# A mixed product scheme for the branch products of a Mamba-2 / merge kernel: three token blocks of 512 and two of 768, weight sums added up by DMAs, order by a list scheduler

## The chip, the cores and the metric

The kernel runs on one core of a Trainium2 chip. The metric is the device time of one execution in microseconds (us). Engines: PE (matmuls; PEld is its weight load), DVE (VectorE), ACT (ScalarE), POOL (GpSimd), SP (SyncE, which here only issues DMAs). Everything is float32.

## The reference, cut to what matters

First a state-space attention: 4 sequences of 768 tokens, 8 heads of 32 columns, state size 16. Its output becomes x, 3072 tokens by 256 columns. Then four branches are merged:

```
p = domain_probs / (domain_probs.sum(-1, keepdims=True) + 1e-09)
for e in range(4):
    h = np.maximum(x @ w1[e], 0.0)           # 256 -> 1024
    out += p[:, e:e + 1] * (h @ w2[e])       # 1024 -> 256
```

## The kernel before

The tokens are 24 chunks of 128, taken in turn from the four sequences. A block is 4 chunks (512 tokens), and there are 6 blocks. The FFN of a block runs over 8 steps (4 branches by 2); a step takes 512 of a branch's 1024 hidden columns. "First" products multiply by w1, "second" products by w2. In pieces of 256 hidden columns, 256 tokens and 128 model columns a step is a 2x2 times 2x2 block matrix product, twice. Instead of 8 block products it makes 7, by Strassen's method in Winograd's form (`fmul`, `smul`). One block product is two matmul instructions of 128x128 by 256 columns, and each float32 matmul leaves two records in the trace.

The price of the saved products is sums on other engines:
- of tokens, four of 128x256 per block on DVE (`sums`, L501 to L504);
- of weights, on POOL in block 0 (`sums_of`, L189 to L193); they are stored in DRAM by DMAs from POOL (L201, L207) and loaded from there by SP in later blocks (L166 and L177 are the loads' lines in `load_w1` and `load_w2`, beside those of the plain weights, L161 and L173);
- of first products: partial results are copied out of a bank by ACT (`snap`, L530), added to another bank by DVE (`total`, L535), then made non-negative and multiplied by the gate p (`gated`, L545);
- of gated results, four differences per step on DVE (`diff`, L552);
- of second products, once per block (`combine`). They stay in four PSUM banks (`acc`) for a whole block.

The first two steps of block 0 (`PLAIN = 2`) use 8 plain products, in `plain_first` (L572) and `plain_second` (L589).

The attention of the next block is woven in. Per chunk: two scans on DVE (`decay_part`, L364), scores on PE (L393), a product with the decays on DVE (`masked`, L405), a small product on POOL that fades the state (L369), for later chunks another on POOL (`cts`, L350), outputs on PE (L450, L462), and copies on ACT.

The order of all of this is written by hand: a loop over n = 2 ... 47 issues one step's first products between the second products of the step before (`fmul`, `smul`). Each engine takes its instructions in that order. SP issues nearly all loads two steps ahead. `finish` writes the end: the last second products in an order of their own, with each result added straight out of its bank, turned by PE and sent.

Of the kernel before, what the change touches and what calls it, by code (L numbers as in the profile page):

```python
# [12 lines left out]
P = 128  # L13
NQ, NT = 4, 2


@with_exitstack
def kernel(
# [10 lines left out]

# [3 lines left out]
    E, DM, F = w1.shape  # L60
    NH = NQ * NT
    HN = P
    BLK = 512
    HB = BLK // 2
    CPB = BLK // P
    NBLK = NCH // CPB
# [4 lines left out]
    FH = F // 2  # L71
    JJ = FH // HB
    SPB = E * JJ
    NS = NBLK * SPB
    assert NBLK == chunks_per_seq

    def real(c):

        return c % CPB * NBLK + c // CPB

    PLAIN = 2
    A12, A22, A11, S3, S1, S2, S4 = range(7)

    const = ctx.enter_context(tc.tile_pool(name="const", bufs=1))
    load = ctx.enter_context(tc.tile_pool(name="load", bufs=3))
    wts = ctx.enter_context(tc.tile_pool(name="wts", bufs=3))
    att = ctx.enter_context(tc.tile_pool(name="att", bufs=2))
    ffn = ctx.enter_context(tc.tile_pool(name="ffn", bufs=2))
    ps_att = ctx.enter_context(tc.tile_pool(name="ps_att", bufs=2, space=bass.MemoryType.PSUM))
    ps_f = ctx.enter_context(tc.tile_pool(name="ps_f", bufs=1, space=bass.MemoryType.PSUM))  # L90
    ps_s = ctx.enter_context(tc.tile_pool(name="ps_s", bufs=1, space=bass.MemoryType.PSUM))
    ctx.enter_context(tc.manual_schedule())


    ac_d = tc.dram_tile([NCH, NH, P], FP32, name="ac_d")
    acut_d = tc.dram_tile([NCH, NH, P], FP32, name="acut_d")
    p_d = tc.dram_tile([T // P, E, P], FP32, name="p_d")
    w1_d = [tc.dram_tile([P, 4, HB], FP32, name=f"w1_d{i}") for i in range(SPB)]
    w2_d = [tc.dram_tile([P, 5 * HB], FP32, name=f"w2_d{i}") for i in range(SPB)]


    st = {}
    SPREAD = 3

    HALF = P // 2

    def turned_round(c):


        return c >= CPB and c % 2 == 1  # L110

    def load_tokens(c):
        xb = load.tile([P, W], FP32, tag="xb", name="xb", bufs=4)
        src = xbc[real(c)]
        if turned_round(c):
            nc.sync.dma_start(out=xb[:, :OBT], in_=src[:, :OBT])
            nc.sync.dma_start(out=xb[:HALF, OBT:], in_=src[HALF:, OBT:])
            nc.sync.dma_start(out=xb[HALF:, OBT:], in_=src[:HALF, OBT:])
        else:
            nc.sync.dma_start(out=xb, in_=src)  # L120
        st.setdefault(c, {})["xb"] = xb

    def load_rows(c):

        xb = load.tile([P, W], FP32, tag="xb", name="xb", bufs=4)
        nc.sync.dma_start(out=xb[:, OBT:], in_=xbc[real(c)][:, OBT:])
        st.setdefault(c, {})["xb"] = xb

    def load_rest(c):
        nc.sync.dma_start(out=st[c]["xb"][:, :OBT], in_=xbc[real(c)][:, :OBT])  # L130

    def load_decays(c):
        ab = load.tile([P, NH * P], FP32, tag="ab", name="ab")
        nc.sync.dma_start(
            out=ab, in_=acut_d[real(c)].rearrange("h s -> (h s)").partition_broadcast(P))
        st.setdefault(c, {})["ab"] = ab

    def load_heads(c):

        ah = st[c]["ah"] = load.tile([HN, P], FP32, tag="ah", name="ah", bufs=4)  # L140
        src = ac_d[real(c)].unsqueeze(1).to_broadcast([NH, N, P])
        if turned_round(c):
            nc.sync.dma_start(out=ah[:HALF], in_=src[NH // 2:])
            nc.sync.dma_start(out=ah[HALF:], in_=src[:NH // 2])
        else:
            nc.sync.dma_start(out=ah, in_=src)

    def load_chunk(c):
        load_tokens(c)
        load_decays(c)  # L150
        load_heads(c)

    wt1, wt2 = {}, {}

    def load_w1(n):
        e, jj = divmod(n % SPB, JJ)
        t1 = wt1[n] = wts.tile([P, 7, HB], FP32, tag="wt1", name="wt1", bufs=5)
        for k in range(2):
            w = 2 - 2 * k
            a_ = 2 if n < SPB or k else 1  # L160
            nc.sync.dma_start(  # L161
                out=t1[:, w:w + a_],
                in_=w1[e, k * P:k * P + P].rearrange("p (a f) -> p a f", a=2)[
                    :, 0:a_, jj * HB:jj * HB + HB])
        if n >= SPB:
            nc.sync.dma_start(out=t1[:, S3:], in_=w1_d[n % SPB])  # L166

    def load_w2(n):
        e, jj = divmod(n % SPB, JJ)
        t2 = wt2[n] = wts.tile([P, 7 * HB], FP32, tag="wt2", name="wt2", bufs=5)  # L170
        for i in range(2) if n < SPB else (1,):
            f = i * FH + jj * HB
            nc.sync.dma_start(  # L173
                out=t2[:, (1 - i) * 2 * HB:(2 - i) * 2 * HB].rearrange("p (j m) -> p j m", j=JJ),
                in_=w2[e, f:f + HB].rearrange("(j p) m -> p j m", p=P))
        if n >= SPB:
            nc.sync.dma_start(out=t2[:, 2 * HB:], in_=w2_d[n % SPB])  # L177

    def w2_op(n, w):

        if w < 4:
            a_, d = divmod(w, 2)
            return wt2[n][:, :4 * HB].rearrange(
                "p (a j d m) -> p a j d m", a=2, j=JJ, d=2)[:, a_, :, d]
        return wt2[n][:, w * HB:w * HB + HB].rearrange("p (j m) -> p j m", j=JJ)

    def sums_of(op, part):
        if part != 1:
            nc.gpsimd.tensor_add(op(S1), op(S3), op(A22))  # L189
            nc.gpsimd.tensor_sub(op(S2), op(S1), op(A11))  # L190
            nc.gpsimd.tensor_sub(op(S4), op(A12), op(S2))
        if part != 0:
            nc.gpsimd.tensor_sub(op(S3), op(A11), op(S3))  # L193

    def sum_w1(n, part=None):


        if n < SPB:
            sums_of(lambda w: wt1[n][:, w].rearrange("p (j m) -> p j m", j=JJ), part)
            if part != 0:  # L200
                nc.gpsimd.dma_start(out=w1_d[n], in_=wt1[n][:, S3:])  # L201

    def sum_w2(n, part=None):
        if n < SPB:
            sums_of(lambda w: w2_op(n, w), part)
            if part != 0:
                nc.gpsimd.dma_start(out=w2_d[n], in_=wt2[n][:, 2 * HB:])  # L207

    pr = const.tile([P, T // P, E], FP32, name="pr")
    a_sb = const.tile([NCH * NH // 2, 2, P], FP32, name="a_sb")  # L210

    a_q = ffn.tile([P, SPREAD, NT, P], FP32, tag="o", name="a_q", bufs=1)
    nc.gpsimd.memset(a_q[:, 0], 0.0)
    one = nc.const_aps.tensor(1.0, [P, 1])
    nc.vector.memset(a_q[:, 1:], 0.0)
    nc.scalar.dma_start(out=pr, in_=probs)
    for queue, c in ((nc.sync, slice(0, 1)), (nc.scalar, slice(1, SPREAD))):
        queue.dma_start(
            out=a_q.rearrange("(q r) c t s -> q r c (t s)", q=NQ)[:, 0, c],
            in_=a.rearrange("(i k) (q t) s -> k q i (t s)", k=NBLK, t=NT)[0][:, c])  # L220
    warm = const.tile([P, 1], FP32, name="warm")
    nc.scalar.mul(warm, one, one)
    load_rows(0)
    nc.sync.dma_start(
        out=a_sb, in_=a.rearrange("c h s -> (c h) s").rearrange("(p r) s -> p r s", r=2))
    load_rows(1)
    load_rest(0)
    load_rest(1)
    load_w1(0)
    load_tokens(2)  # L230


    ident = const.tile([P, NQ, P], FP32, name="ident")
# [4 lines left out]
    tmask = const.tile([P, NT], FP32, name="tmask")  # L238
# [5 lines left out]
    zeros = const.tile([P, P], FP32, name="zeros")  # L244
    nc.vector.memset(zeros, 0.0)

    qmask = const.tile([P, NQ, D], FP32, name="qmask")
# [3 lines left out]

    own = const.tile([P, 1], FP32, name="own")
# [6 lines left out]


    def clip_first(engine, c):
        clip(engine, a_q[:, c].rearrange("p c t s -> p (c t s)"), own)
        engine.memset(a_q[:, c, :, 0:1], 0.0)

    clip_first(nc.vector, slice(0, 1))


    pairs = const.tile([P, T // P, 2], FP32, name="pairs")
# [4 lines left out]

    nc.vector.reciprocal(total_p, total_p)
    nc.gpsimd.tensor_mul(pr, pr, total_p.to_broadcast([P, T // P, E]))
    clip_first(nc.vector, slice(1, SPREAD))

    clip(nc.gpsimd, a_sb)

# [9 lines left out]
    gate = {}  # L289

    def turn_gates(pool, tag):

        rows = T // P * E
        pp = pool.tile([rows, P], FP32, tag=tag, name="pp")
        nc.tensor.transpose(pp, pr.rearrange("p i e -> p (i e)"), ident[:, 0])
        p_sb = const.tile([rows, P], FP32, name="p_sb")
        gate["rows"] = p_sb
        nc.scalar.copy(out=p_sb, in_=pp)  # L298

    def store_gates():  # L300
        nc.sync.dma_start(out=p_d.rearrange("i e s -> (i e) s"), in_=gate["rows"])

    def spread_gate(pool, tag):

        p_sb = gate["rows"]
        g = pool.tile([P, CPB, P], FP32, tag=tag, name="gp")
        for i in range(CPB):
            r = real(i) * E
            nc.tensor.matmul(  # L309
# [663 lines left out]
```

## Time and profile before

| | |
|---|---|
| three timed runs | 637.74, 638.09, 638.25 us |
| median | 638.09 us |
| span of the profiled execution, first to last instruction | 636.4 us |
| ACT busy in the span | 119.7 us |
| POOL busy in the span | 112.9 us |
| moved by DMA | 121.61 MB, mean 191 GB/s |
| granted TensorE clock | 1.000 |

The span is that of one execution under the profiler, and its own time outside the span is not listed, so 638.09 - 636.4 = 1.7 us is taken for what lies around it. A group line names the line of the code, the engine, the operation, output <- inputs, the shape and a count; then busy us, mean ns of one, and the idle time of the engine just before, with what ended it. Durations of matmuls overlap, because they are pipelined: the distance between starts is their price.

### The profile page before, as it was taken

What the parts mean: (1) busy time and instruction counts of PE and PEld (TensorE: products, weight loads), DVE (VectorE), ACT (ScalarE), POOL (GpSimd) and SP (SyncE); (2) the same over time, 40 slices, a digit from 0 to 9 for tenths busy, and PEclk for the clock granted to TensorE, in tenths of its full rate; (3) what the DMA queues carried; (4) which work ended last, traced back from release to release, by engine and by line L of the source; (5) the groups of instructions that cost most, each with busy time, mean ns of one, the idle gap of its engine ahead of it and who ended that gap; (6) DMA issues with size and microseconds to landing.
All of it is one profiled execution on the core that took longest, in us unless ns stands there. A gap on an engine that the chain in (4) does not pass through costs nothing.

```text
span 636.4 us, 9259 instructions
## 1 busy us (share of the span) xinstructions
PE 631.9 (99%) x3405; PEld 538.2 (85%) x3405; DVE 483.4 (76%) x810; ACT 119.7 (19%) x264; POOL 112.9 (18%) x164
## 2 busy tenths in 40 slices
PE   9999999999999999999999999999999999999997
PEld 5888888888888888888888888888888888888886
DVE  7868999887787788678687778778867677756555
ACT  4011221212111221122211221122111211111110
POOL 6788557020000002000002000000100000100001
PEclk9999999999999999999999999999999999999999
DMA  6998894745666392757284566639365644167001
GB/s 188 302 357 295 282 346 156 279 169 166 191 200 238 90 366 81 228 175 248 99 287 149 168 199 196 231 102 358 89 220 162 242 160 133 61 152 241 2 1 33
DMA packets 98513, 121.61 MB, mean 191 GB/s; under 512 B 29529, under 2 KB 81957, under 8 KB 98469
## 3 DMA queue, kind: packets, MB, share of 16 engines
q1 hardware_dynamic: 95512, 111.20, 53.7%
q0 software_dynamic: 2432, 9.50, 3.8%
q8 instruction: 27, 0.44, 0.3%
q10 hardware_dynamic: 524, 0.32, 0.2%
q14 instruction: 18, 0.14, 0.1%
HBM read 108.16 MB, written 12.83 MB: 190 GB/s over the span
## 4 chain that ended last, share of the span: by engine, by line
PE 99%; ACT 0%; DVE 0%; issue 0%
PE acc L608 44%; PE X L523 25%; PE Y L523 19%; PE acc L589 2%; PE g L393 2%; PE y L462 2%; PE X L572 1%; PE Y L572 1%; PE y L450 1%; PE t L729 1%; PE a L331 0%; PE y L428 0%; PE gp L309 0%; PE turned L655 0%; DVE o L686 0%; ACT p_sb L298 0%
## 5 line engine op out<-in xcount | busy, mean ns | idle before, releaser
L535 DVE TENSOR_TENSOR z<-Y,snap 128x512 f32<-128x512 f32 x138 | 94.6, 686 | 117.6 <-ACT snap L530 66.7
L608 PE MATMUL acc<-hT,wt 128*128 128x256 f32 x736 | 181.1, 379 | 0.0
L530 ACT COPY snap<-X 128x512 f32<-128x512 f32 x138 | 80.8, 586 | 464.2 <-PE X L523 403.5
L608 PEld LDWEIGHTS acc<-hT,wt 128*128 128x128 f32 x736 | 140.1, 190 | 18.7
L608 PE MATMUL acc<-h,wt 128*128 128x256 f32 x552 | 142.6, 381 | 0.0
L523 PE MATMUL X<-yS,wt 128*128 128x256 f32 x552 | 141.8, 380 | 0.0
L608 PEld LDWEIGHTS acc<-h,wt 128*128 128x128 f32 x552 | 104.2, 190 | 16.8 <-issue 2.3
L523 PEld LDWEIGHTS X<-yS,wt 128*128 128x128 f32 x552 | 105.0, 190 | 14.3 <-issue 0.3
L545 DVE SCALAR_TENSOR_TENSOR h<-z,gate 128x512 f32<-128x512 f32 x138 | 99.9, 724 | 3.5 <-PE acc L589 0.4
L523 PE MATMUL Y<-yT,wt 128*128 128x256 f32 x368 | 94.5, 379 | 0.0
L523 PEld LDWEIGHTS Y<-yT,wt 128*128 128x128 f32 x368 | 68.9, 190 | 10.5
L552 DVE TENSOR_TENSOR hT<-h,hT 128x512 f32<-128x512 f32 x92 | 65.2, 709 | 1.8
L552 DVE TENSOR_TENSOR hT<-h,h 128x512 f32<-128x512 f32 x92 | 65.1, 748 | 1.4
L364 DVE TENSOR_TENSOR_SCAN LT<-ab,ident 128x512 f32<-128x512 f32 x42 | 52.1, 1242 | 0.0
L523 PE MATMUL Y<-yS,wt 128*128 128x256 f32 x184 | 48.3, 385 | 0.0
L523 PE MATMUL X<-yT,wt 128*128 128x256 f32 x184 | 47.3, 379 | 0.0
L369 POOL TENSOR_TENSOR MT<-xb,LT 128x128 f32<-128x128 f32 x20 | 8.6, 428 | 205.4 <-PE Y L523 68.8
L405 DVE TENSOR_TENSOR MT<-g,LT 128x256 f32<-128x256 f32 x93 | 32.0, 415 | 11.5 <-PE g L393 11.4
L523 PEld LDWEIGHTS Y<-yS,wt 128*128 128x128 f32 x184 | 34.2, 190 | 6.4 <-issue 2.2
L523 PEld LDWEIGHTS X<-yT,wt 128*128 128x128 f32 x184 | 35.0, 190 | 4.7
L545 DVE SCALAR_TENSOR_TENSOR h<-X,gate 128x512 f32<-128x512 f32 x50 | 34.2, 684 | 5.0 <-PE X L523 3.4
L350 POOL TENSOR_TENSOR cts<-ctm,dec 128x256 f32<-128x256 f32 x20 | 14.1, 726 | 128.3 <-DVE dec L347 128.3
(103 smaller groups left out, 325.2 us busy)
## 6 DMA issues: line engine op xcount, KB each, us to landing
wt<-in_w_dram SPq DMA_DIRECT2D x112, 256.0 KB
wt<-w_d SPq DMA_DIRECT2D x40, 640.0 KB
wt<-w_d SPq DMA_DIRECT2D x40, 512.0 KB
ab<-acut_d SPq DMA_DIRECT2D x21, 512.0 KB
gate<-p_d SPq DMA_DIRECT2D x23, 256.0 KB
w_d<-wt POOLq DMA_DIRECT2D x8, 640.0 KB, 3.7
wt<-in_w_dram SPq DMA_DIRECT2D x40, 128.0 KB
w_d<-wt POOLq DMA_DIRECT2D x8, 512.0 KB, 7.7
```

Of the source, the lines that this page charges most:

```text
L350: nc.gpsimd.tensor_mul(cts, s["ctm"], dec.unsqueeze(1).to_broadcast([HN, NT, P]))
L364: nc.vector.tensor_tensor_scan(out=LT[:, i * w:i * w + w], data0=s["a"][i], data1=ident.rearrange("p h s -> p (h s)")[:, :w], initial=0.0, ...
L393: nc.tensor.matmul(out=g.rearrange("p t s -> p (t s)"), lhsT=s["xb"][k, OBT:OBT + P], rhs=s["ctm"][k].rearrange("p t s -> p (t s)"), start ...
L405: nc.vector.tensor_mul(s["MT"][:, h, 0:P], s["g"][q], s["LT"][:, h])
L462: nc.tensor.matmul(out=y[32 * q:32 * q + 32, t, 0:w], lhsT=s["xb"][:, h * D:h * D + D], rhs=s["MT"][:, NT * q + t, 0:w], start=(k == 0 and ...
L523: nc.tensor.matmul(out=f[bank][:, j], lhsT=wt1[n][:, w, j * P:j * P + P], rhs=rhs, start=(i in (1, 2, 5) and j == 0), stop=(j == JJ - 1), ...
L530: nc.scalar.copy(out=s, in_=first[n]["X"])
L535: nc.vector.tensor_add(z, first[n]["Y"], first[n][i])
L545: nc.vector.scalar_tensor_tensor(out=h, in0=first[n][src], scalar=0.0, in1=g.unsqueeze(1).to_broadcast([P, JJ, HB]), op0=ALU.max, op1=ALU. ...
L552: nc.vector.tensor_sub(h[o], h[x], h[y])
L572: nc.tensor.matmul(out=f[bank][:, j], lhsT=wt1[n][:, w, j * P:j * P + P], rhs=yT[k][:, i, cols], start=(i == 0 and j == 0), stop=(i == 1), ...
L608: nc.tensor.matmul(out=acc[k, u][:, half], lhsT=w2_op(n, w)[:, j], rhs=rhs[:, j], start=(begins and j == 0), stop=(n % SPB == SPB - 1 and ...
```

## The change

Lines with L from here on are those of the changed kernel.

- **Blocks.** 24 chunks become three blocks of 4 chunks (scheme `B`, 2x2x2 in 7 products for 8) and two of 6 chunks (scheme `H`). `H` takes 768 hidden columns and 768 tokens at a time, 3x2 pieces of weights times 2x3 of tokens and back, in 15 products for 18, with 10 sums of weights, 12 of tokens, and in each group 7 sums with a bank and 16 of SBUF tiles. A branch pair's 1024 x 4 columns are 16 pieces of 256: five groups of three, and piece 0 plainly. Block 0 has 4 pieces (one branch) plainly.
- **Banks.** All 8 banks are one pool. A running sum is continued in a bank that ACT fills first (`seed`, L837), and saved by ACT (`snap`, L832; `visit`, L1096 and L1099). Second products no longer keep four banks for a block: `visit` takes one bank for a "house" of two results, seeds it, adds the products of that group, and copies it back to SBUF.
- **Weight sums.** Those of `B` are made on DVE or POOL (L930) and stored by SP (L935). Those of `H` are made in DRAM: a DMA of SP copies one summand (L893), then a DMA of POOL adds the other (L896, L901; a sum of sums waits for the one before). Ten chains (5 groups by 2 weights) of ten sums go one by one with the 11 units of the first three blocks. A unit is two groups of `B` or one of `H`.
- **Order.** Each operation is entered in a `Plan` with its engine (some with DVE or POOL), an expected duration, what it reads and writes. PE's order is given: first products of a unit interleaved with second products of the unit before (`put`), scores after the unit's first product (SC = 1) and outputs after the 14th (OUT = 14). `Plan.run` fills the other engines by due time, gives out the buffers and the banks, and decides DVE or POOL. The instructions are issued in the order of planned starts.
- **End.** The last group's second products run alone, by house (`LATE`); each house is copied to SBUF and the results are added there, turned by PE and sent (`leave_last`).
- The products' line is L823, the gates' L858, other sums of large tiles L850, L976, L1001 and L1146, the fading product L454, `cts` L731, scores L436, outputs L461 and L767, weight loads L411, L417 and L927.

```diff
-    ORDER = (1, 3, 7, 5, 6, 2, 4)
...
-    for n in range(PLAIN, NS):
...
-        opened(n)
-        total(n, 1, "11")
-        gated(n, "11", "z11")
...
+ORDER = B, B, B, H, H
...
+    def add(self, on, fn, reads=(), writes=(), part=(), lag=0.0, due=None, reuse=None, two=False,
+            port=True, after=None):
...
+            e = min(t, key=lambda e: t[e])
+            now = t[e]
...
+                if len(w.on) > 1 and e == "POOL":
+                    if max(ready, now) + w.on[e] > w.latest + late + SLACK or self.backlog(
+                            waiting["DVE"], now, t["DVE"], w) < BACK:
+                        continue
+                rank = w.latest
...
+    homes = {
+        "V": some(NV, [P, 2, FB], "v"),
+        "W": some(NW, [P, 2 * FB], "w"),
+        "bank": some(8, [P, 512], "bank", psum),
...
+    def product(bank, half, w, x, start):
+
+        for j in range(JJ):
+            o = bank.rearrange("p (a m) -> p a m", a=2)[:, j if half is None else half]
+            nc.tensor.matmul(
+                out=o, lhsT=w[:, j], rhs=x if half is None else x[:, j],
+                start=(start and j == 0), stop=(j == 1), skip_group_check=True)
...
+    def sums_by_dma(scheme, fbs, l, after, due):
...
+            dma(lambda e, r=r, f=f, i=i: nc.sync.dma_start(
+                out=split(slot[r]), in_=source(fbs[f], l, i)), 1, 300, writes=[v], due=due, after=after)
+            if y in sums:
+                plan.add({"POOL": 1.0}, lambda e, r=r, y=y: nc.gpsimd.dma_start(
+                    out=slot[r], in_=slot[y], accum_op=ALU.add), port=False, lag=ACC,
+                    reads=[sums[y]], part=[v], due=due, after=after)
+            else:
+                g, h = scheme.blocks[l][y]
+                plan.add({"POOL": 1.0}, lambda e, r=r, g=g, h=h: nc.gpsimd.dma_start(
+                    out=split(slot[r]), in_=source(fbs[g], l, h), accum_op=ALU.add), port=False,
+                    lag=ACC, part=[v], due=due, after=after, reads=[v])
...
+    def threes_first(k, fbs):
...
+        b7 = mul(7)
+        s7 = snap(b7)
+        s12 = snap(mul(12))
+        mul(11, b7)
+        a12 = combine(b7, s12, -1)
+        gate(2, 0, mul(0, seed(s7)))
+        b6 = mul(6)
+        t67 = combine(snap(b6), s7, -1)
+        b3 = mul(3)
+        s3 = snap(b3)
+        b5 = mul(5, seed(a12))
+        gate(2, 2, b5)
+        mul(2, b7)
+        gate(1, 2, combine(b7, s12, -1))
+        mul(10, b3)
+        v = combine(b3, s12, -1)
...
+    def visit(k, house, terms, last=False):
...
+        bank = seed(held, size) if held is not None else value("bank", fills=both)
...
+        v = kept[k, house] = value("V")
+        v.both = both
+        if both:
+            act(.6, lambda e: nc.scalar.copy(out=flat(v), in_=bank.t), reads=[bank], writes=[v])
...
+    def leave_last(k, O, order):
...
+            tails.append(plan.add({"PE": .35}, turn, reads=[o], writes=[t]))
+            act(.4, lambda e, t=t, r=r: nc.scalar.copy(out=r.t[:, 0], in_=t.t[:, :2 * P]),
+                reads=[t], writes=[r])
...
+        merged = put(behind, seq) if behind else seq
...
+        for n in range(per if u in early_units else 0):
+            if early:
+                sums_by_dma(H, *early.pop(0), merged[0], lambda w=merged[-1]: w)
...
+    done = plan.run(line, now, {"PE": now, "DVE": now - .6, "ACT": now + 1.0, "POOL": now - 2.0,
+                                "SP": now + .4})
+    for w in done:
+        w.fn(w.by)
```

## The prediction

> **What bounds the kernel now.** I read the page's busy line first, then the chain that ended last, then the chain's pieces in order of time, and last the busy time by stage.
>
> ```profile
> span 636.4 us, 9259 instructions
> PE 631.9 (99%) x3405; PEld 538.2 (85%) x3405; DVE 483.4 (76%) x810; ACT 119.7 (19%) x264; POOL 112.9 (18%) x164
> ...
> PE 99%; ACT 0%; DVE 0%; issue 0%
> ```
>
> PE is busy nearly all the time and it is also 99% of the chain. So no wait needs removing: only less PE work can shorten this kernel, and only new PE waits can lengthen it. The chain's pieces give the price of that work:
>
> ```profile
> 587.29 2.59 PE acc L608 x12
> 599.38 2.59 PE acc L608 x12
> 611.47 2.59 PE acc L608 x12
> ...
> 631.54 0.88 PE acc L608 x4
> 632.42 0.02 issue
> 632.44 0.43 DVE o L686
> 632.88 0.04 issue
> 632.92 0.45 PE turned L655 x2
> 633.38 0.02 issue
> 633.40 0.27 ACT rows L692
> ```
>
> One step (7 first and 7 second products) returns every 12.09 us, so one product is 12.09/14 = 0.863 us; the piece 2.59 us x12 says the same (two instructions of a product leave four records, 4 x 0.216). The last six lines are the end: after the last product an add, two transposes, a copy and a DMA. The span ends at 636.4; the three timed runs have a median of 638.09, so 1.7 us lie around the span. I add all changes to 638.1.
>
> **What is removed on PE.** By instruction counts of the two programs, the products are 1,352 matmuls before (L523 and L608 644 each, L572 and L589 32 each) and 1,328 after (all L823), two to a product: 676 against 664. By blocks: 116 + 112 + 112 in the three blocks of 512 and 162 each in the two of 768 (2 x (5 x 15 + 6)). The attention matmuls are equal (96 scores, 192 outputs and 40 of the state in both programs). Saved: 12 x 0.863 = 10.4 us, and all of it stood on the chain. Floor: 638.1 - 10.4 = 627.7.
>
> **What is added at the end.** Before, the add read the bank directly. After, the last house (0,7) is copied from its bank to SBUF by ACT (L530's 128x512 copy: 0.586), then two results follow it instead of one: add 0.42, add 0.42, transposes 0.45; ACT copies and sends the first result (0.37 + 0.36), then copies the second (0.37). That puts the last copy's end about 2.65 us after the last product; before it is 633.67 - 632.42 = 1.25. So +1.4 us.
>
> **What is added beside PE: VectorE.** These rows price it:
>
> ```profile
> L545 DVE SCALAR_TENSOR_TENSOR h<-z,gate 128x512 f32<-128x512 f32 x138 | 99.9, 724 | 3.5 <-PE acc L589 0.4
> L535 DVE TENSOR_TENSOR z<-Y,snap 128x512 f32<-128x512 f32 x138 | 94.6, 686 | 117.6 <-ACT snap L530 66.7 <-PE Y L523 50.8
> L552 DVE TENSOR_TENSOR hT<-h,hT 128x512 f32<-128x512 f32 x92 | 65.2, 709 | 1.8
> L530 ACT COPY snap<-X 128x512 f32<-128x512 f32 x138 | 80.8, 586 | 464.2 <-PE X L523 403.5 <-DVE MT L405 60.8
> ```
>
> A group of the 15-product scheme has 9 gates (7 from a bank at 0.686, 2 from SBUF at 0.724 = 6.3 us), 7 sums with a bank at 0.686 (4.8) and 16 sums of SBUF tiles at 0.73 (11.7): 22.8 us if all stay on DVE, beside 30 products = 25.9 us of PE. That is 88%, before attention. The scheduler puts 62 of the 270 SBUF sums of the whole program on POOL. Cutting DVE's order of instructions at the gates and pricing each by its row gives, for the five groups of the first large block, 24.6, 25.4, 25.9, 22.9 and 23.5 us; PE has 25.9 us of products each and 8.3 us of attention (6 chunks x 1.38, from the chain's shares 2.1% g and 3.1% y of 636.4 us over 24 chunks) spread over the first three, so up to 28.7. The second large block has 20.6 to 23.8 against 25.9. In the blocks of 512 a unit of 28 products (24.2 us, 27.0 with a pair of chunks) meets 13.4 to 26.5 us. All together 535 us on DVE, against 483: more, but in no stage more than PE.
>
> POOL's adds slow DVE's. The trace shows it where POOL makes the weight sums:
>
> ```profile
> L552 DVE TENSOR_TENSOR hT<-h,h x10: 683/1100/1212, 66.2 to 118.2; 128x512 f32<-128x512 f32 x10
> L552 DVE TENSOR_TENSOR hT<-h,hT x8: 683/692/1209, 69.7 to 109.8; 128x512 f32<-128x512 f32 x8
> ```
>
> (shortest, median, longest in ns). The median of the first form is 0.42 us above its floor; some 18 x 0.25 = 4.5 us were lost beside 31 us of POOL work between 62 and 110 us, 0.15 us per us of POOL. After, POOL has 62 adds of 128x512 (no row shows one; two of 128x256 at 0.725 = 1.45 at the least, at 1.009 = 2.0 at the most) and some 82 small operations, about 147 us: 21 us of DVE in all, about 1 us per large group. That leaves DVE at 27 of 28.7 us in the tightest group. So I take no steady loss, but a needed result can come one operation late. Bounds for PE: 0 (PE now idles 0.3 us) and one operation (0.73 us) in each of the 10 large groups, 7 us; I take 2 us, nearer the row of today, since by the code four other products stand between most sums and their readers.
>
> [...]
>
> **ACT** makes some 400 copies of 128x512 (banks seeded and saved) at 0.586: 235 us, with the rest 280 us, 45%. A large group has about 25 of them, 14.7 of 25.9 us. Hidden; what it can do is part of the 2 us.
>
> **The adding DMAs.** 100 plain copies (SP) and 100 adds (POOL), 128 KB each, run during the three blocks of 512. Two limits:
>
> ```profile
> 13.28:62.00 48.72, 48.72 (x269) 40.63 (x268) 38.87 (x55) 7.53 (x22) 38.61 (x51) 1.00 0.91 310
> 62.00:110.00 48.00, 48.00 (x296) 40.48 (x296) 45.32 (x70) 9.72 (x24) 30.86 (x38) 1.00 0.71 261
> 110.00:620.00 510.00, 510.00 (x2696) 439.74 (x2695) 380.36 (x636) 94.47 (x198) 31.90 (x48) 1.00 0.55 178
> ```
>
> (PE, PEld, DVE, ACT, POOL busy, then clock, DMA share, GB/s.) At 0.91 busy and 310 GB/s the supply is about 340 GB/s, and PE lost nothing. Demand until the large blocks: 184 tiles of weights loaded or stored (48.2 MB), copies and adds 26.2, attention, gates and output 18.6: 93 MB in 340 x 0.863 + 16 x 1.38 = 315 us, 295 GB/s or 87%. Nothing in the trace shows an add; if one costs two transfers, 106 MB, 337 GB/s, 99%, still no loss; if three, 119 MB need 351 us, +36 us. I take one to two, cost 0, because a whole unit of weights is loaded ahead.
>
> The other limit is landing. A chain of sums is five adds deep, the next chain's first adds are issued ahead of the last one, and each unit holds one chain: POOL needs four landings and four issues of 0.6 us per unit of 26 to 27 us, so a landing L of up to 6.0 us is free. Behind a waiting add stand POOL's L454 and L731, without which PE's output matmuls can't start. The rows: 16 KB to DRAM from POOL 1.8 us; 512 and 640 KB stores of weight sums 2.9/6.2/9.8 (shortest, median, longest), medians 7.7 and 3.7 by size. Ends: 1.8 to 9.8. I take 3.7: five times fewer bytes than that row, but two reads. Cost 0. [...]
>
> **Sum:** 638.1 - 10.4 + 1.4 + 2 = **631.1 us**.
>
> **Rivals.**
> 1. Crowding on DVE and ACT (17 in 100). PE misses one operation in every large group and, now and then, in the small ones: 629.1 + 7 + 2 = 638. [...] Against: no stage sum exceeds PE's. I share it 10 faster, 6 no change, 1 slower.
> 2. Slower: the adds land late (12 in 100). It decides at L = 6.0 us, on POOL's queue. At 6.5 us a chain takes 28.4 us for 26.5, ten chains 19 us: 650; at the 7.7 us of the 512 KB row 33.2, +67 us: about 698. For it: the median of 6.2 in a stage as loaded as this one will be. Against: those transfers are four to five times larger.
> 3. Slower: an add costs three transfers (7 in 100): weights late in the first half, 631 + 36 = 667.
> 4. Fewer waits and a shorter end than I count (2 in 100): 627.6.
>
> That the products are not fewer is no rival: the counts settle it. The forecast has 62 in 100.
>
> **Numbers.** 0.2% (1.3 us) is about what a measurement of this kernel can tell from no change. Faster 62 + 10 + 2 = 74, no change 6, slower 1 + 12 + 7 = 20. The range goes from the floor less 0.2, 627.5, up through rival 1 and the start of rivals 2 and 3 to 645 (landings up to 6.35 us); about 14 in 100 lie above it and 1 below.
>
> **What would show each step.** The product's price: L823 at 0.216 us per record and 664 products. The end: ACT's copy, two adds and transposes after the last product, 4.0 us becoming about 5.4. The crowding: PE idle before L823 put down to DVE or ACT, in the second half. The adds: landing of L896 and L901 against 6.0 us, PE idle before L461 put down to POOL's L454 or L731, and DMA share near 1 in the first half with PE waiting for w. I am wrong if PE idles more than about 10 us, or if a product costs other than 0.863.

## The result, and the profile after

The changed kernel takes 703.2 us (four runs, 700.1 to 709.3) against 638.2: a ratio of 1.103, interval 1.098 to 1.108. It is slower by 65 us; the forecast was 631.1 us and faster.

The page of the changed kernel, same parts as before:

```profile
span 700.5 us, 10392 instructions
PE 642.3 (92%) x3363; PEld 538.9 (77%) x3363; DVE 514.9 (74%) x869; ACT 269.8 (39%) x552; POOL 241.2 (34%) x264
PE   9799699899997498995697999999999999999996
PEclk9999699999998799999799999999999999999998
DMA  7999999999999999998999674756445553682001
...
q0 software_dynamic: 16320, 13.11, 13.7%
...
w_d<-w_d POOLq DMA_DIRECT2D x70, 128.0 KB, 6.0
...
w_d<-in_w_dram POOLq DMA_DIRECT2D x30, 128.0 KB, 6.8
```

The first row of digits is the key: PE has holes (4, 5, 6) only in the first 22 of 40 slices, and there the DMA row stands at 8 or 9. After about 400 us PE has none. The clock row has its low digits (6 to 8) in the same slices as PE's holes. The last two lines are the adding DMAs: they land 6.0 and 6.8 us after their issue.

Busy time by stage, in the columns named in the prediction:

```profile
60.00:80.00 20.00, 12.83 (x59) 9.17 (x57) 11.60 (x22) 1.87 (x5) 10.73 (x14) 0.80 1.03 300
220.00:240.00 20.00, 10.88 (x41) 8.90 (x40) 5.63 (x10) 5.98 (x11) 7.67 (x11) 0.76 1.11 321
320.00:340.00 20.00, 7.21 (x39) 5.12 (x39) 10.58 (x21) 3.94 (x9) 6.39 (x7) 0.79 0.87 243
...
480.00:500.00 20.00, 20.00 (x126) 16.97 (x125) 13.34 (x22) 9.82 (x20) 4.57 (x3) 1.00 0.44 133
500.00:520.00 20.00, 20.00 (x95) 17.60 (x94) 16.30 (x27) 10.32 (x19) 0.00 (x0) 1.00 0.55 181
```

In the worst stages PE works 7 to 13 of 20 us, DVE is idle too, and the clock falls to 0.76 to 0.80. In the large blocks PE works 20.00 of 20. Summed over the stages from 20 to 400 us PE is idle for 51 us; its busy time there, weighted by one minus the clock, gives an estimate of 18 us lost to the lower clock.

What ended PE's idle time between 13 and 400 us (us in total, times, longest us; the five smaller rows add 8.5 us):

```profile
PE bank L823 <- ACT v L832: 14.8, 2, 12.2
PE bank L823 <- POOL v L850: 14.7, 3, 9.1
PE bank L823 <- DVE v L858: 13.4, 6, 5.2
```

The chain that ended last shows what stood behind the two longest of these waits (start, us, what):

```profile
219.23 9.24 DMA w_d<-w_d
...
229.68 6.09 DMA w_d<-w_d
...
236.59 1.56 POOL v L850
238.19 7.61 PE bank L823 x24
...
332.31 4.81 DMA xb<-in_xbc_dram
...
337.51 0.39 ACT ctm L429
337.89 0.48 ACT v L832
338.41 9.63 PE bank L823 x36
```

So PE stood 9.1 us because a sum on POOL (L850) came behind adding DMAs that waited for one another to land, and 12.2 us because ACT waited for a late load of tokens (`xb`) with its copy behind.

The end:

```profile
669.92 22.89 PE bank L823 x106
...
692.89 0.59 ACT v L1096
693.47 1.47 ACT v L1216 x5
694.95 0.04 issue
694.99 0.37 ACT v L1216
```

From the last product (692.8) to the end of the span 7.7 us pass; before it was 4.0. So span against span: -10.4 (12 products) + 3.7 (end) + 51 (idle PE) + 18 (clock) = +62, of 64.1 seen; the other 2 us are not accounted for.

### The profile page after: what moved, and what is told of

The parts are those of the page before. It is cut to its first block, busy times and chain, and to the rows that moved or that the text cites. A ratio compares the mean times of both kernels' runs of the same rounds, so it can differ in the third digit from the quotient of the medians.

```text
span 700.5 us, 10392 instructions
## 1 busy us (share of the span) xinstructions
PE 642.3 (92%) x3363; PEld 538.9 (77%) x3363; DVE 514.9 (74%) x869; ACT 269.8 (39%) x552; POOL 241.2 (34%) x264
## 3 DMA queue, kind: packets, MB, share of 16 engines
q0 software_dynamic: 16320, 13.11, 13.7%
HBM read 136.21 MB, written 37.99 MB: 249 GB/s over the span
## 4 chain that ended last, share of the span: by engine, by line
PE 69%; DMA 17%; DVE 5%; issue 4%; POOL 2%; SPq 1%; ACT 1%; POOLq 0%; ACTq 0%; DVEq 0%
PE bank L823 67%; DMA w<-in_w_dram 5%; DMA w<-w_d 3%; DMA xb<-in_xbc_dram 2%; DMA w_d<-w_d 2%; DVE v L850 2%; PE bank L461 1%; DMA gate<-p_d 1%; DVE v L858 1%; DMA w_d<-in_w_dram 1%; DMA ab<-acut_d 1%; DMA acut_d<-a_cut 1%; DVE LT L448 1%; PE bank L436 1%; POOL v L850 1%
## 5 line engine op out<-in xcount | busy, mean ns | idle before, releaser
L823 PE MATMUL bank<-v,w 128*128 128x256 f32 x1864 | 455.3, 389 | 36.4 <-POOL v L850 14.7
L823 PEld LDWEIGHTS bank<-v,w 128*128 128x128 f32 x1864 | 360.0, 195 | 99.1 <-DVE v L858 16.3
L823 PE MATMUL bank<-Y,w 128*128 128x256 f32 x792 | 205.7, 383 | 14.8 <-ACT v L832 14.8
L850 DVE TENSOR_TENSOR v<-v,v 128x512 f32<-128x512 f32 x208 | 157.6, 778 | 46.4 <-POOL v L850 33.5
L823 PEld LDWEIGHTS bank<-Y,w 128*128 128x128 f32 x792 | 151.9, 192 | 37.0 <-ACT v L832 15.9
L850 POOL TENSOR_TENSOR v<-v,v 128x512 f32<-128x512 f32 x62 | 91.8, 1489 | 186.2 <-DVE v L858 143.7
L858 DVE SCALAR_TENSOR_TENSOR v<-bank,gate 128x512 f32<-128x512 f32 x172 | 117.4, 685 | 51.8 <-PE bank L823 48.0
L1096 ACT COPY v<-bank 128x512 f32<-128x512 f32 x114 | 66.8, 586 | 176.5 <-PE bank L823 176.2
L837 ACT COPY bank<-v 128x512 f32<-128x512 f32 (+1 forms) x196 | 109.8, 577 | 42.4 <-DVE v L850 17.7
L832 ACT COPY v<-bank 128x512 f32<-128x512 f32 x106 | 62.0, 586 | 114.9 <-PE bank L823 114.2
L896 POOL DMA_DIRECT2D w_d<-w_d x70 | 62.4, 986 | 104.9 <-DMA w_d<-w_d 69.1
L901 POOL DMA_DIRECT2D w_d<-in_w_dram x30 | 31.7, 1138 | 85.1 <-DMA w_d<-in_w_dram 84.9
L850 DVE TENSOR_TENSOR v<-bank,v 128x512 f32<-128x512 f32 x40 | 27.5, 688 | 19.9 <-PE bank L823 19.7
L429 ACT ACTIVATE ctm<-xb,tmask 128x128 f32<-128x128 f32 x48 | 16.1, 393 | 54.1 <-DMA xb<-in_xbc_dram 37.2
L731 POOL TENSOR_TENSOR cts<-ctm,dec 128x256 f32<-128x256 f32 x20 | 23.2, 1261 | 19.8 <-PE bank L767 11.5
L1146 DVE TENSOR_TENSOR v<-v,v 128x256 f32<-128x256 f32 x49 | 20.5, 457 | 9.9 <-ACT v L1096 9.8
L930 DVE TENSOR_TENSOR w<-w,w 128x256 f32<-128x256 f32 x28 | 18.3, 674 | 9.3 <-DMA w<-in_w_dram 8.1
L1146 POOL TENSOR_TENSOR v<-v,v 128x256 f32<-128x256 f32 x17 | 15.0, 902 | 21.4 <-ACT v L1096 21.3
L930 POOL TENSOR_TENSOR w<-w,w 128x256 f32<-128x256 f32 x20 | 19.5, 1044 | 0.1
L1001 DVE TENSOR_TENSOR bank<-bank,v 128x512 f32<-128x512 f32 x22 | 15.2, 693 | 5.2 <-PE bank L823 5.2
```

The source lines that it names most:

```text
L823: nc.tensor.matmul(out=o, lhsT=w[:, j], rhs=x if half is None else x[:, j], start=(start and j == 0), stop=(j == 1), skip_group_check=True)
L832: act(.6, lambda e: nc.scalar.copy(out=flat(v), in_=bank.t), reads=[bank], writes=[v])
L837: act(.6 if to > FB else .38, lambda e: nc.scalar.copy(out=bank.t[:, :to], in_=flat(v)[:, :to]), reads=[v], writes=[bank])
L850: plan.add(engines, lambda e: (on(e).tensor_add if sign > 0 else on(e).tensor_sub)(flat(v), whole(x), whole(y)), reads=[x, y], writes=[v], ...
L858: dve(.7 if x.kind == "bank" else .74, lambda e: nc.vector.scalar_tensor_tensor(out=h.t, in0=whole(x).rearrange("p (j m) -> p j m", j=JJ), ...
L896: plan.add({"POOL": 1.0}, lambda e, r=r, y=y: nc.gpsimd.dma_start(out=slot[r], in_=slot[y], accum_op=ALU.add), port=False, lag=ACC, reads= ...
```

## The experiments

Two theories. **Bandwidth:** the packets of the copies and adds fill the DMA engines in the first 380 us, and loads that PE needs land late. **Queue:** POOL stands at each add until the add before it has landed, and the work behind it is late. Every kernel below is the changed one with the edit shown.

**e1_no_sums**: neither copies nor adds.

```diff
-            dma(lambda e, r=r, f=f, i=i: nc.sync.dma_start(
-                out=split(slot[r]), in_=source(fbs[f], l, i)), 1, 300, writes=[v], due=due, after=after)
+            dma(lambda e: None, 1, 300, writes=[v], due=due, after=after)
...
-                    out=slot[r], in_=slot[y], accum_op=ALU.add), port=False, lag=ACC,
+                plan.add({"POOL": 1.0}, lambda e: None, port=False, lag=ACC,
```

> Left out: the weight sums of the large blocks. Neither the 100 copies nor the 100 adding DMAs are issued, and the large blocks load plain weights of the same size in place of the sums; every engine's order is otherwise that of the changed kernel. Bandwidth theory (the sums' packets fill the DMA engines for the first 380 us, so loads land late) and queue theory (POOL stands at an add until the one before has landed, and its adds for PE stand behind): both 629 to 635 us, the prediction's sum. Third theory (loads of the first block, crowded DVE or cold clock cost time by themselves): over 640.

637.7 us, ratio to the kernel before 0.9993 (0.9984 to 1.0003). All 65.5 us go with the sums' DMAs, but without them the change is still only even, between the ranges of the theories. The first block shows part of why; POOL's, ACT's and PE's timelines there and the stage:

```profile
27.60 0.72 POOL L928 TENSOR_TENSOR w<-w 128x256 f32<-128x256 f32 x1 [10.47 <-DMA w<-in_w_dram]
28.28 0.41 POOL L454 TENSOR_TENSOR MT<-xb,LT 128x128 f32<-128x128 f32 x1
...
23.98 0.69 ACT L429 ACTIVATE ctm<-xb,tmask 128x128 f32<-128x128 f32 x2 [9.01 <-DMA xb<-in_xbc_dram]
...
25.65 2.94 PE L823 MATMUL bank<-v,w 128*128 128x256 f32 x8 [4.24 <-ACT A L471]
```

```profile
20.00:40.00 20.00, 15.61 (x78) 12.33 (x77) 11.87 (x18) 2.93 (x10) 4.88 (x7) 0.91 0.95 289
40.00:60.00 20.00, 20.00 (x136) 16.46 (x135) 19.90 (x39) 8.20 (x19) 9.77 (x13) 1.00 0.99 328
```

POOL waited 10.5 us for a weight load, in front of the fading product that PE's outputs need, and ACT 9.0 us for a load of tokens, in front of a copy that PE needs. PE is idle 4.4 us, of which 4.24 ended with ACT and only 0.16 with POOL, and its clock stands at 0.91 for that stage.

**e2_copies_only** and **e3_plain_pool**: the adds left out; the adds as plain writes.

```diff
-                    out=slot[r], in_=slot[y], accum_op=ALU.add), port=False, lag=ACC,
+                    out=slot[r], in_=slot[y]), port=False, lag=ACC,
```

> Left out: the 100 adding DMAs (the stored rows hold one summand). SP's 100 copies of 128 KB stay. Queue theory: 629 to 636 us, as POOL waits for no landing. Bandwidth theory: the adds' packets took 1.51 ms of 16 engines' time, 95 us, and go; demand falls to about 0.85 of the supply: 631 to 645.

> POOL's 100 adding DMAs overwrite instead of adding (the sums are left out); their number, bytes and waits stay. A 1 KB packet of an add took about 112 ns, one of a plain transfer 52, so the DMA engines are relieved of about 50 us. Bandwidth theory: 640 to 660 us. Queue theory: five waits for a landing per chain remain, landing falls from 6 to about 5 us: 670 to 700.

657.7 and 678.2 us, one run each. The first lies above both ranges; the second lies in the queue theory's range and above the bandwidth theory's. So the bill has three parts: copies 20.0, POOL's transfers 20.4, their adding 25.0. Each part holds all that comes with it: in e2 POOL stands at none of the sums' transfers, in e3 for 164 us. Their price in DMA time is on the pages' queue lines (packets, MB, share of 16 engines' span), of the run without sums, with copies, and with plain transfers:

```profile
q1 hardware_dynamic: 119332, 121.17, 60.5%
```

```profile
q1 hardware_dynamic: 127332, 134.28, 64.6%
```

```profile
q0 software_dynamic: 4800, 13.11, 6.1%
```

0.646 x 655.9 - 0.605 x 635.5 = 39 us for the copies, 0.061 x 676.2 = 41 us for the plain transfers, and 0.137 x 700.5 = 96 us for the adds. The same 13.11 MB cost an add 2.3 times a plain transfer, in 3.4 times as many packets.

**e4_no_chain**: no add waits for another.

```diff
-                    out=slot[r], in_=slot[y], accum_op=ALU.add), port=False, lag=ACC,
+                    out=split(slot[r]), in_=source(fbs[0], l, 0), accum_op=ALU.add), port=False, lag=ACC,
```

> Every adding DMA takes its second summand from the plain weights, so none waits for another add, only for its own copy (the sums are wrong ones). Number and bytes stay. Queue theory: 635 to 660 us. Bandwidth theory: 690 to 710, as before the edit.

713.9 us, above both ranges: adds from the plain weights come in 20,800 packets instead of 16,320, and landing is 9.0 us in the median, so the run changed more than the waits. POOL waits for no add any more, but it still stands 140.7 us at adds whose copy by SP has not landed, against 154.0 us for copies and adds in the changed kernel. So leaving out the wait of add for add brings nothing back; POOL's standing at adds was hardly less.

**e8_acc9**: the same question from the other side.

```diff
-ACC = 5.0
+ACC = 9.0
```

> Nothing left out. The planner is told that an adding DMA lands 9 us after its issue (ACC 9 instead of 5; measured 6.0 and 6.8 us), so POOL's order puts other work between the adds of a chain. Queue theory: most of the 65 us come back, 640 to 670 us. Bandwidth theory: the same packets in the same stage, 690 to 710 us.

704.2 us, in the bandwidth theory's range. A planner that is told of a later landing doesn't help. But the queue is not gone either: POOL stands at adds for 157.2 us (122.5 for copies, 34.7 for adds). PE's longest wait in this run, followed back (lines of PE, DVE and POOL):

```profile
217.91 1.12 PE L767 MATMUL bank<-cts,M 64*64 64x256 f32 x4 [16.45 <-DVE v L858]
...
215.45 0.69 DVE L850 TENSOR_TENSOR v<-v,v 128x512 f32<-128x512 f32 x1 [20.35 <-POOL v L850]
...
212.96 1.17 POOL L901 DMA_DIRECT2D w_d<-in_w_dram  x1 [24.03 <-DMA w_d<-in_w_dram]
```

POOL stood 24.0 us at an add for its copy, with a sum behind it that DVE needed, and PE needed DVE. Three waits of this form are 29.7 of the 55.5 us that PE is idle here between 20 and 400 us. So neither theory falls. e2 shows that transfers cost 20 us with no add on POOL's queue; how the other 45 us divide between full DMA engines and POOL's queue stays open.

**e5_late_chains**: chains spread into the first large block, and each load of sums meant to wait for its sums.

```diff
+CHAINS_AT = 2, 4, 6, 8, 9, 10, 11, 12, 12, 13
...
-        for n in range(per if u in early_units else 0):
+        for n in range(CHAINS_AT.count(u)):
```

> Nothing left out. The ten chains of adding DMAs are spread over units 2 to 13, four of them into the first large block, where DMA share was 0.4 to 0.8 in the changed kernel, instead of one per unit from the start. Bandwidth theory: the 65 us that the chains cost fall by about the four in ten that leave the full stage: 670 to 685 us. Queue theory: each chain still holds POOL for about 5 landings, and in the large block POOL has adds of its own that PE waits for: 695 to 715.

692.5 us, between both expectations. (Not every row of its sums is the reference's; it is read for its transfers and times.) In the large block the stage 440 to 460 us shows what a chain does there:

```profile
440.00:460.00 20.00, 7.07 (x34) 5.89 (x32) 6.75 (x14) 4.32 (x8) 10.72 (x11) 0.77 1.08 276
460.00:480.00 20.00, 20.00 (x125) 16.12 (x125) 13.85 (x25) 8.36 (x16) 6.56 (x6) 0.89 0.63 164
...
459.23 0.69 DVE L851 TENSOR_TENSOR v<-v,bank 128x512 f32<-128x512 f32 x1 [13.12 <-POOL v L851]
```

DMA share 1.08 and PE idle, in a stage with share 0.80 in the changed kernel. PE's longest wait there, 12.9 us, ended with the DVE sum of the last line, and POOL, for which that sum waited, had stood 12.2 and 4.1 us at adds: both theories' signs in one stage. A chain costs 5.5 us in the mean ((692.5 - 637.7)/10), against 6.6 in the changed kernel, and its price in DMA time, (39 + 96)/10 = 13.5 us, is half a unit. So moving four chains of ten brought back 11 of 65 us.

**e6_engine_sums**, **e9_engine_fade**, **e11_pool_sums**: no DMA sums; the first large block makes its weight sums on DVE and POOL (e6), with the fading product of chunk 3 on DVE (e9), or on POOL alone (e11).

```diff
-    early = [((3 * g + 1, 3 * g + 2, 3 * g + 3), l) for g in range(NG) for l in (1, 2)]
+    early = []
...
-                plan.add(B256, lambda e, r=r, x=x, y=y, sign=sign: (
+                plan.add({"POOL": .78} if scheme is H else B256, lambda e, r=r, x=x, y=y, sign=sign: (
```

> Nothing left out. The weight sums of the first large block are made by DVE and POOL from loaded weights and stored by SP, as those of the small blocks are; no copies in DRAM, no adding DMAs. DMA falls by 26 MB to about 122 MB, the 637.7 us of the run without sums; 100 sums of 128x256 go on the engines in the first large block (45 on DVE at 0.42 = 3.8 us per group, on 24.4 of 26 to 28.7). Bandwidth theory: 638 to 648 us. If instead the stage of the small blocks is slow by itself: over 650.

> Nothing left out. Sums of the first large block on the engines, and the fading product of chunk 3 on DVE, together. If the two causes add up: 5 to 7 us less than the run with sums on the engines alone, 632 to 642 us.

> Nothing left out. The weight sums of the first large block on POOL alone, none on DVE (on both they gave 654.1 us, with DVE busy 19 to 20 of 20 us from 380 to 440 us). If DVE was the bound there: 638 to 646 us. If POOL's adds of 0.78 us each, in turn with DVE's two-input sums, are the bound: 650 or more.

654.1, 652.7 (ratio 1.0227, 1.0210 to 1.0244) and 658.4 us. From 40 us on the small blocks are clean in e6, and the loss has moved into the first large block:

```profile
400.00:420.00 20.00, 18.60 (x94) 15.30 (x95) 18.07 (x26) 8.86 (x17) 14.92 (x16) 1.00 0.45 156
420.00:440.00 20.00, 11.38 (x76) 8.07 (x74) 19.62 (x42) 4.83 (x9) 2.16 (x3) 0.81 0.44 153
```

DVE works 19.6 of 20 us there and PE waits for it; DMA is half idle. So in that block DVE has no room for the 45 sums more that it got there. POOL alone is no better: e11, where DVE has no weight sum of that block, takes 658.4. What happens there can be read in e12 below, which has the block's sums on POOL too. From 360 to 400 us POOL works 19.86 and 17.50 of 20 us, DVE's own sums of SBUF tiles (L850) take 1.11 us each in the chain, and three in a row 3.38, against a median of 0.69 in the changed kernel, and DVE is as full (19.06 and 19.76 of 20).

**e7_no_sums_fade** and **e13_no_sums_both**: what is left over in e1.

```diff
-            plan.add({"POOL": .43}, lambda e: fade(c, s["MT"].t, s["xb"].t, s["LT"].t),
+            plan.add({"DVE" if c == 3 else "POOL": .43}, lambda e: fade(
+                c, s["MT"].t, s["xb"].t, s["LT"].t, on(e)),
```

```diff
-LANDING = 2.2
+LANDING = 5.0
...
-    line.extend(put(behind) + tails)
+    ending_ = put(behind)
+    line.extend(ending_[:-2] + tails[:2] + ending_[-2:] + tails[2:])
```

> Left out: the weight sums of the large blocks, as in the run without sums. One product more is moved: the fading product of chunk 3 goes from POOL to DVE, since in the run without sums POOL stood 10.5 us at a weight sum for its load (17.1 to 27.6 us) with that product behind it, PE idled 4.4 us and its clock stood at 0.91 for 20 us. If the queue in front of that product explains what is left over the prediction's 631: 630 to 633 us. If it is a general slowness: 636 to 638.

> Left out: the weight sums of the large blocks, as in the run without sums (637.7 us). Two edits beside: the planner is told that a load lands 5.0 us (and its bytes) after its issue instead of 2.2, so that waits for loads are not put in front of work that PE needs in the first block (there 3.9 to 4.4 us of idle PE and about 1.5 us of cold clock), and the end sends each result with one DMA, mostly from SP, with two of six results turned ahead of the last product (the end takes 7.3 us after the last product, 4.0 in the kernel before). If these two are all that separates the change from its 627.7: 629 to 631.5 us. If something general is slow: 634 to 638.

e7: 636.8 us (0.9982, 0.9971 to 0.9993). Its edit took POOL's wait away, and 0.9 us of the median with it. The other wait, which had stood beside it in e1, is still there: ACT stands 8.7 us at a mask (L429) for its load of tokens, with the copy that PE waits for behind it. Both are waits for loads that land later than the planner believes (2.2 us and the bytes; in e7's chain a weight load takes 4.93 us and the load of tokens behind it 4.97). e13, which corrects that belief, takes 635.9 us in the median (0.9966, 0.9947 to 0.9984), with executions from 631.5 to 637.6. So its median lies in the range that its expectation gave to a general slowness. The profiled one is its fastest:

```profile
0.00:20.00 20.00, 18.72 (x141) 11.10 (x142) 16.39 (x47) 8.06 (x25) 7.79 (x24) 1.00 0.75 233
20.00:40.00 20.00, 20.00 (x117) 16.72 (x116) 14.71 (x25) 3.90 (x12) 7.57 (x12) 1.00 1.00 324
40.00:620.00 580.00, 580.00 (x3089) 498.77 (x3087) 459.67 (x785) 254.50 (x508) 151.65 (x136) 1.00 0.61 191
```

PE has no hole from 20 to 620 us, and its last product ends at 624.4. Less 2.5 us of two results turned early (0.75) and PE's wait for them (1.8), that is 621.9, where the prediction's step 632.4 - 10.4 puts it at 622.0. So in this execution, with the sums paid for by nobody, the scheme works as priced. Why other executions of the same kernel take up to 6 us more was not tried; the seven slower ones record a clock of 0.993 to 0.997 (e1 with its hole: 0.996), the three fastest 0.998 to 1.000.

**e12_all**: POOL's sums, that belief and that end together.

> Nothing left out. Sums of the first large block on POOL alone, loads planned at 5.0 us, and the shorter end, together. If the parts add up (the run with POOL's sums less about 5.5 and 2): 631 to 639 us.

650.0 us (1.0186, 1.0171 to 1.0201). The weight sums on engines cost some 14 to 21 us wherever I put them (650.0 against 635.9 in e13, 658.4 against 637.7 in e1), and the scheme saves 10.4. No version that makes its sums beats the kernel before.

## Why the prediction was wrong, step by step

- **The product, 12 x 0.863 us: right.** In the profiled execution of e13 the last product ends within 0.2 us of it.
- **The end, +1.4: right in kind, +3.7 measured.** I let ACT send the first result before it copies the second. All six pairs of transposes stand after the last product in PE's order, ACT copies all six first (1.84 us) and then issues six DMAs in a row.
- **Crowding on DVE and ACT, 2 us: too much.** From 430 to 680 us PE idles for 0. DVE's sums of SBUF tiles took 778 ns in the mean (726 in e1, with as many of POOL's adds), within DVE's room. Where POOL made the weight sums of the first large block, in e12, they took 1.11 to 1.13 us each in the chain from 387 to 393 us, and DVE had no room (19.76 us of 20).
- **The adding DMAs, 0: this step failed.** The sums' DMAs cost 65.5 us (e1). The step weighed them by bytes at the best supply seen (340 GB/s) and took one or two transfers for an add. Measured, an add costs 2.3 transfers of engine time, and the share is about 1.0 for 300 us. Worse was the second half: that up to 99% demand costs nothing because a unit of weights is loaded ahead. The copies alone, with no add, already cost 20 us, at a mean share of 0.82 from 60 to 380 us (e1: 0.69). PE needs more than weights: SP issues the loads of tokens, decays and gates of the attention too, and an engine that stands at a late one has other work behind it in its order. In the changed kernel PE's longest wait (12.2 us) ended behind a load of tokens, and in e2 too (9.2 us).
- **Landing, 3.7 us and cost 0: measured 6.0 and 6.8, and this step failed too.** I took the row of the large stores by size; the row by load (median 6.2) was the nearer one. The two reads that I gave an add were my estimate, and the pages don't show them: HBM read is 136.21 MB with the adds and with plain transfers in their place (e3). The issue, 0.6 us in the sum, took 0.82 and 1.09. So POOL's queue was at or over the limit of 6.0 us that the prediction had worked out, and the sum had no wait for the copies, at which POOL stood 84.9 us. 14.7 us of PE's idle time ended with a sum of POOL's behind adds; it was L850, not L454 or L731. How much of the 65.5 us is this queue's, the runs don't settle (e4 and e8 left POOL standing). Rival 2 had this mechanism, but its 698 us, near the result, is luck: that takes a landing of 7.7 us, and at the measured 6.0 to 6.8 its own sum gives 631 to 662. Rival 3 had the full DMA engines and too small a price: 667 at three transfers for an add, and some 9 us at the measured 2.3. It had no copies that cost, and no lower clock.
- **The first block: not seen.** I compared sums by stage, and its DVE sum was fine. POOL and ACT stood at loads (10.5 and 9.0 us in e1), because the list scheduler had put these waits in front of what PE needs. The changed program's order has a wait for a load ahead of L454, which could have been read off.
- **The clock: not priced.** In the six stages of the changed kernel from 20 to 400 us in which PE missed more than 3.5 of 20 us the granted clock was 0.76 to 0.91. Over all stages there that is an estimated 18 us beside 51 us of idle PE, about a third of a us for each.

## What to carry to other kernels

Where a change moves work to DMA, price it in time of the DMA engines by the kind of transfer, not in bytes, and add it to each stage's share: here copies that raised the mean share from 0.69 to 0.82 cost 20 us, though the weights were loaded a unit ahead. And look at what stands in its engine's queue behind each transfer that waits. Work that is moved off an engine with no room must go to one that has room in the same stage; if all three places (DMA, DVE, POOL) cost more than the products saved, fewer products aren't fewer us. And in an order made by a planner, look for waits on loads ahead of work that the bound engine needs.

## What the runs showed of the hardware

An adding DMA of 128 KB within DRAM took 2.3 times the engine time of a plain one of the same shape (96 against 41 us for a hundred), and cut its bytes into 16,320 packets where the plain one had 4,800. DMA share in a 20 us stage went over 1 in eight stages with adds (1.02 to 1.11, at 252 to 342 GB/s), and in one stage of e1 without them (1.06 at 339 GB/s). DVE's sums of two SBUF tiles took 726 ns in the mean in e1 and 784 in e6, where POOL made 80 weight sums instead of 25. In the changed kernel the stages with 7 to 13 us of PE's work in 20 had a granted clock of 0.76 to 0.80, and those from 400 to 680 us, with 20.00 of 20, had 1.00.
